# The third matrix of a gated MLP as seven half-size products, and its units streamed from DRAM

## The chip, the cores and the metric

One core of one Trainium2 chip runs the whole program. The metric is device time in microseconds of one launch. Engines as a profile names them: PE (TensorE, matmuls), PEld (its weight loads), DVE (VectorE), ACT (ScalarE), POOL (GpSimd), SP (SyncE, which issues all transfers here).

## The reference, cut to what matters

Three stages run one after the other on 4 batches. Each batch gives 512 tokens and 32 rows of a small state, 544 rows of width 512 in all.

```python
# 1: attention between x (4, 8, 512, 64) and state (4, 8, 32, 64), both ways, concatenated -> (2176, 512)
h = x @ w_in                        # 2: (512 -> 2048)
x = h * tanh(softplus(h)) @ w_out   #    Mish, (2048 -> 512)
xn = x / rms(x) * rms_g             # 3: RMS norm, then a gated MLP
g, val = xn @ w_gate, xn @ w_val    #    (512 -> 1536) twice
out = (g * sigmoid(g) * val) @ w_out2   # (1536 -> 512)
```

The MLP matrices arrive as 64-bit floats, the result is 32-bit.

## The kernel before, in words

**Numbers.** Every operand of a large product is kept as two 16-bit halves, a high and a low one, after a power-of-two scale. A product is three matmuls: high·high, high·low, low·high. A weight is loaded as 64-bit words, put together on DVE and ACT, measured (`norms`: squares on ACT), scaled by `pow2` (one tiny PE matmul against `ones`, line 468, and six tiny DVE operations), and split (`split`: high on either engine, low on DVE, line 590).

**Tiling.** Tokens run in five chunks: four of 512 columns (c = 0 to 3) and one of 128 (c = 4, the state rows of all batches). Matrices are cut into units of 512 of the inner width: u = 0 to 3 in the Mish MLP (`group`, `l2`: groups g0 to g8), u = 0 to 2 in the gated one.

**Gated MLP.** For each chunk and unit, `quad` computes the gate product and then the value product. Each is a 512 x 512 by 512 x 512 product, done as seven products of 256 x 256 blocks instead of eight: weight blocks W11, T2, T1, T3, W21, W22, T4 (and W12 for the small chunk), token blocks A11, S2, S1, A12, S3, A22, S4. One such half-size product is 12 matmuls of 256 columns (line 1088). Three banks of PSUM (pool `p`, four banks) are used per quad, one of them three times; five DVE additions (line 1100) combine them. Then ACT takes Silu (line 1126), DVE multiplies by the value (line 1134), and the result is split into a high part (`gh`, line 457 or 455) and a low part (`gl`, line 1138).

**The last matrix** (w_out2, `w2`) is `l3`, line 1200: for each unit, four output banks `a0` to `a3`, each 12 matmuls of 512 columns, accumulated over the three units. Before, all of `w2` lies in SBUF.

**Weights on the way.** The gate and value matrices are prepared during the Mish MLP in a region of `psm`, then stored to DRAM (`keep`) and loaded back (`load`) to where they stay: unit 0 in `attm`, unit 1 in `w1`, unit 2 in `w2m`, `w2` in `psm`. `attm` is attention's memory, `w1` and `w2m` hold the Mish matrices until these are done.

**Order.** Nothing is issued in the order of the code. Each step is an `op` with its reads, writes, engine choices and an assumed cost; `Plan.order` runs a list schedule over them, ten times, and each engine's instructions are then emitted in that order. `at` and `due` are due times that `chains` spreads backwards, and pools (`p`, `t`, `g`, `a0` ...) limit how far one step may be ahead of another. On the chip the order is fixed: an instruction that is not ready holds up all behind it on its engine. This holds for PE and for SP's one queue of transfers as well.

Of the kernel before, what the change touches and what calls it, by code (L numbers as in the profile page):

```python
# [22 lines left out]
XX, XW, XN, XK = 15, 14, 9, 22  # L23
# [8 lines left out]
class Op:  # L32
    __slots__ = (
        "engs", "fn", "deps", "succ", "bufs", "tab", "at", "due", "reserve", "lat", "name", "spare")


class Plan:
# [15 lines left out]
    def __init__(self, nc):  # L53
        self.nc, self.spare = nc, None
# [14 lines left out]
    def op(self, engs, fn, r=(), w=(), tab=None, at=None, reserve=0, lat=0.0, after=(), due=None, name=""):  # L69
        o = Op()  # L70
        o.engs, o.fn, o.tab, o.at, o.due, o.reserve, o.lat, o.name = engs, fn, tab, at, due, reserve, lat, name
        o.spare = self.SPARE if self.spare is None else self.spare
# [69 lines left out]
    def chains(self):  # L142
# [7 lines left out]
        for o in reversed(self.ops):  # L150
            cost = min(o.engs.values())
            cost = cost + o.lat if "T" in o.engs else (1.0 if "D" in o.engs else o.spare) * cost + o.lat
# [164 lines left out]
def attn_moe_moe_kernel(  # L317
# [74 lines left out]
    prep = Mem("", 0, psm, 2048)  # L392

    home, rest = {}, {}
# [16 lines left out]
    P.fifo.update(("t", "g", "xb", "xt", "t2", "t3", "sbt"))  # L411
    P.pool("t", [tt(512 * k, 512) for k in range(10)])
    P.pool("g", [gm(512 * k, 512, F16).rearrange("p (l f) -> p l f", l=2) for k in range(6)])
    P.pool("sx", [sxm(512 * k, 512) for k in range(2)])
# [4 lines left out]
    P.pool("raw2", stage[:1])  # L419
    sb = attm(0, 2048).rearrange("p (b g h d) -> p b g h d", b=B, g=2, h=4)  # L420
# [23 lines left out]
    def part(w, u, j, a):  # L444

        m, at = rest[w, u] if j == 7 else (home[w, u][0], home[w, u][1] + 512 * j)
        return m(at + 256 * a, 256, F16)

    def part_names(w, u, js):
        m, at = home[w, u]  # L450
        return [n for j in js for n in (rest[w, u][0].names(rest[w, u][1], 512) if j == 7 else m.names(at + 512 * j, 512))]
# [12 lines left out]
    def pow2(part, pname, k, floor, nm, xexp):  # L464
# [4 lines left out]
           r=[pname], w=[b], reserve=0, name=f"pow2 {nm}")  # L469
        t, q, s, si = small([128, k]), small([128, k], I32), small([128, k]), small([128, k])  # L470
        z = small([128, k], I32)

        def fn(e):
            nc.vector.tensor_scalar(t, P[b][:, :k], floor, 2.0, ALU.max, ALU.mult)
# [6 lines left out]
        op({"V": 0.93}, fn, r=[b], w=[(nm, "s")], name=f"pow2 {nm}")  # L481
# [84 lines left out]
    def norms(pairs, nm, xexp, who):  # L566


        part, tot = small([128, 2]), small([128, 1])
        for i, (ap, ns) in enumerate(pairs):  # L570
            q = buf(fresh("junk"), "junk")

            def fn(e, i=i, ap=ap, q=q):
                nc.scalar.activation(  # L574
                    P[q].rearrange("p (a n) -> p a n", a=2), ap, ACTF.Square, accum_out=part[:, i:i + 1])

            op({"A": a_sb(1024) + 0.17}, fn, r=ns, w=[q, (nm, "n", i)], name=f"sq {who}")
        op({"V": 0.13}, lambda e: nc.vector.tensor_tensor(tot, part[:, 0:1], part[:, 1:2], ALU.add),
           r=[(nm, "n", 0), (nm, "n", 1)], w=[(nm, "t")])
        return pow2(tot, (nm, "t"), 1, 2.0 ** -10, nm, xexp)[0]  # L580
# [12 lines left out]
    def plain(w, u, m, at, xexp, pool="raw", after=()):  # L593
# [4 lines left out]
        def dn(k):  # L598
# [4 lines left out]
                   for i in range(2)], (w, u), xexp, f"{w}{u}")  # L603
# [6 lines left out]
    def seven(w, u, m, at, pool, after=()):  # L610
# [18 lines left out]
        for k in range(4):  # L629
# [3 lines left out]
        def both(a, b):  # L633
            return m(at + 256 + 512 * a, 512 * (b - a + 1)).rearrange("p (x f) -> p x f", f=512)[:, ::b - a, :]

        s = norms([(both(W11, W12), qn(W11, W12)), (both(W21, W22), qn(W21, W22))], (w, u), XW, f"{w}{u}")
# [17 lines left out]
    def state_scale():  # L654
# [10 lines left out]
        s, si = pow2(part, "xpart", B, 2.0 ** -50, "x", XX)  # L665
# [159 lines left out]
    def sread_scale(due):  # L825
# [7 lines left out]
        s, si = pow2(part, "x4part", 1, 2.0 ** -50, "x4", XX)  # L833
# [284 lines left out]
    def gated(c):  # L1118
        oa = [buf(("oa", c, t), f"a{t}") for t in range(4)]
        for u in range(U2):  # L1120
            c3, kap = sc[f"c3{u}"], sc[f"kap{u}"]
            A, c12, c21, c22 = quad(c, u, "wg")
            s11 = buf(fresh("s"), "t")
            ss = []
            for k, (i, o) in enumerate(((A, s11), (c12, c12), (c21, c21), (c22, c22))):
                op({"A": a_ps(512) + 0.09}, lambda e, i=i, o=o, c3=c3: nc.scalar.activation(  # L1126
                    P[o], P[i], ACTF.Silu, scale=c3), r=[i, f"c3{u}"], w=[o], tab="silu", name="silu")
                ss.append(o)
            flush2()
            vs = quad(c, u, "wv")  # L1130
            gs = []
            for s, v in zip(ss, vs):
                g = buf(fresh("g"), "g")
                op({"V": v1(512) + 0.06}, lambda e, s=s, v=v, kap=kap: nc.vector.scalar_tensor_tensor(
# [232 lines left out]
```

## Time and profile before

| | |
|---|---|
| median of 3 runs | 810.72 us (808.15 to 813.57) |
| the profiled execution, its own time | 811.83 us |
| its span, first to last instruction | 810.1 us |
| PE busy | 784.5 us (97%), 5362 matmuls |
| DVE busy | 596.1 us (74%) |
| ACT busy | 373.9 us (46%) |
| mean granted TensorE clock | 0.981 |
| moved by the transfers | 76.86 MB |

An engine that is busy 97% of the span need not be the bound everywhere, and an idle engine is not free where one of its results is awaited. So the rows below go stage by stage: how busy each engine is there, what PE waited for, and how long one operation takes when the next follows at once.

### The profile page before, as it was taken

What the parts mean: (1) busy time and instruction counts of PE and PEld (TensorE: products, weight loads), DVE (VectorE), ACT (ScalarE), POOL (GpSimd) and SP (SyncE); (2) the same over time, 40 slices, a digit from 0 to 9 for tenths busy, and PEclk for the clock granted to TensorE, in tenths of its full rate; (3) what the DMA queues carried; (4) which work ended last, traced back from release to release, by engine and by line L of the source; (5) the groups of instructions that cost most, each with busy time, mean ns of one, the idle gap of its engine ahead of it and who ended that gap; (6) DMA issues with size and microseconds to landing.
All of it is one profiled execution on the core that took longest, in us unless ns stands there. A gap on an engine that the chain in (4) does not pass through costs nothing.

```text
span 810.1 us, 13000 instructions
## 1 busy us (share of the span) xinstructions
PE 784.5 (97%) x5362; PEld 481.5 (59%) x5362; DVE 596.1 (74%) x1237; ACT 373.9 (46%) x617; POOL 1.6 (0%) x7
## 2 busy tenths in 40 slices
PE   6799999999999999999999999999999999999996
PEld 4344454544444445754457767776776777777673
DVE  5999999989998868688556896458666784645532
ACT  6999898943644635556444542113410340211200
POOL 0000000000000000000000000000000000000000
PEclk9589999999999999999999999999999999999998
DMA  8654614102242731525473210011001000010010
GB/s 221 206 158 156 228 48 142 53 1 108 101 179 120 299 154 55 209 104 195 156 286 143 86 72 1 1 53 53 1 2 53 27 1 1 2 53 1 1 40 27
DMA packets 31983, 76.86 MB, mean 95 GB/s; under 512 B 19508, under 2 KB 19508, under 8 KB 29108
## 3 DMA queue, kind: packets, MB, share of 16 engines
q1 hardware_dynamic: 31924, 76.03, 26.7%
q8 instruction: 42, 0.69, 0.3%
q14 instruction: 17, 0.14, 0.0%
HBM read 55.84 MB, written 20.19 MB: 94 GB/s over the span
## 4 chain that ended last, share of the span: by engine, by line
PE 69%; DVE 12%; ACT 9%; DMA 8%; issue 1%; SPq 0%; ACTq 0%; DVEq 0%
PE p L1088 27%; PE a L1200 16%; PE a L940 11%; PE p L903 9%; DMA psm<-in_moe_w_out_dram 3%; PE p L1166 2%; ACT sxm L549 2%; DVE psm L590 2%; DMA psm<-in_moe_w_gate_dram 1%; DMA psm<-in_moe_w_val_dram 1%; ACT junk L574 1%; DVE g L918 1%; DVE psm L459 1%; DMA kept_wg<-psm 1%; PE a L1266 1%
## 5 line engine op out<-in xcount | busy, mean ns | idle before, releaser
L940 PE MATMUL a<-g,w2m 128*128 128x512 f16 (+1 forms) x960 | 185.7, 347 | 0.4 <-ACT slot L455 0.4
L903 PE MATMUL p<-slot,w 128*128 128x512 f16 (+1 forms) x960 | 184.7, 348 | 0.0
L1100 DVE TENSOR_TENSOR tt<-p,tt 128x512 f32<-128x512 f32 x120 | 82.5, 689 | 80.4 <-PE p L1088 79.8
L903 PEld LDWEIGHTS <-w 128*128 128x128 f16 x960 | 85.6, 98 | 91.5 <-issue 2.9
L1200 PE MATMUL a<-psm,g 128*128 128x512 f16 x612 | 138.0, 379 | 0.0
L940 PEld LDWEIGHTS <-w2m 128*128 128x128 f16 x960 | 85.7, 99 | 87.8 <-issue 3.1
L1200 PEld LDWEIGHTS <-g 128*128 128x128 f16 x612 | 59.7, 98 | 64.5
L1088 PEld LDWEIGHTS <-w2m 128*128 128x128 f16 x672 | 65.7, 98 | 11.3
L1088 PEld LDWEIGHTS <-w 128*128 128x128 f16 x672 | 65.7, 98 | 11.2 <-issue 1.7
L1088 PEld LDWEIGHTS <-attm 128*128 128x128 f16 x672 | 65.7, 98 | 10.3
L914 ACT ACTIVATE tt<-p,page 128x512 f32<-128x512 f32 x68 | 45.6, 673 | 32.6 <-PE p L903 32.4
L455 ACT ACTIVATE g<-tt 128x512 f16<-128x512 f32 x24 | 14.7, 626 | 89.2 <-PE a L1200 45.5
L918 DVE SCALAR_TENSOR_TENSOR g<-tt,page,g 128x512 f16<-128x512 f32 x68 | 50.7, 748 | 3.0 <-ACT g L455 2.1
L590 DVE SCALAR_TENSOR_TENSOR psm<-psm,page 128x512 f16<-128x512 f32 x60 | 45.0, 750 | 4.3 <-ACT psm L455 2.1
L1126 ACT ACTIVATE tt<-tt,page 128x512 f32<-128x512 f32 x36 | 25.9, 721 | 47.6 <-DVE tt L1100 47.6
L549 ACT ACTIVATE sxm<-psm 128x512 uint16<-128x512 uint16 x58 | 43.4, 773 | 9.6 <-DMA psm<-in_moe_w_out_dram 6.0
L1088 PE MATMUL p<-slot,attm 128*128 128x256 f16 x384 | 46.5, 273 | 0.0
L1088 PE MATMUL p<-slot,w2m 128*128 128x256 f16 x384 | 46.3, 273 | 0.0
L1088 PE MATMUL p<-slot,w 128*128 128x256 f16 x384 | 46.0, 273 | 0.0
L455 ACT ACTIVATE psm<-psm,page 128x512 f16<-128x512 f32 (+1 forms) x37 | 26.2, 717 | 30.4 <-DVE psm L590 23.4
L544 DVE TENSOR_SCALAR sxm<-psm 128x512 uint16<-128x512 uint16 x68 | 28.2, 453 | 11.8 <-DMA psm<-in_moe_w_out_dram 7.5
L1138 DVE TENSOR_TENSOR g<-tt,g 128x512 f16<-128x512 f32 x48 | 31.9, 689 | 1.3 <-ACT g L455 0.2
(182 smaller groups left out, 906.5 us busy)
## 6 DMA issues: line engine op xcount, KB each, us to landing
psm<-in_moe_w_out_dram SPq DMA_DIRECT2D x14, 1024.0 KB, 5.0
psm<-in_moe_w_in_dram SPq DMA_DIRECT2D x8, 1024.0 KB, 5.3
psm<-in_moe_w_gate_dram SPq DMA_DIRECT2D x6, 1024.0 KB, 5.2
psm<-in_moe_w_val_dram SPq DMA_DIRECT2D x6, 1024.0 KB, 5.2
kept_wg<-psm SPq DMA_DIRECT2D x3, 2048.0 KB, 7.0
kept_wv<-psm SPq DMA_DIRECT2D x3, 2048.0 KB, 7.9
out_dram<-slot SPq DMA_DIRECT2D x4, 1024.0 KB, 3.8
attm<-in_x_dram SPq DMA_DIRECT2D x24, 128.0 KB, 3.1
```

The costliest lines, as they stand in the source:

```text
L455: nc.scalar.activation(o, i, ACTF.Copy, scale=1.0 if scale is None else scale)
L544: nc.vector.tensor_scalar(s16[:, :, 1], r16[:, :, 3], 0x8000, None, ALU.bitwise_and)
L549: nc.scalar.activation(s16[:, :, 0], r16[:, :, 1], ACTF.Copy, scale=2.0 ** -13, bias=2.0 ** -14 - 0.5)
L590: op({"V": v1(512)}, lambda e: nc.vector.scalar_tensor_tensor(lo, f, s, h, ALU.mult, ALU.subtract), r=[*fn_, *hn, sname], w=ln, name=f"sl ...
L903: nc.tensor.matmul(P[ph][:, i * n:(i + 1) * n], part("wi", u, k, a)[:, f * 128:(f + 1) * 128], xh[:, k, b, :], start=m == 0, stop=m == 3 * ...
L914: op({"A": a_ps(512) + 0.09}, lambda e, s=s, ph=ph, ce=ce: nc.scalar.activation(P[s], P[ph], ACTF.Mish, scale=ce), r=[ph, f"ce{c}_{u}"], w ...
L918: op({"V": v1(512) + 0.06}, lambda e, s=s, g=g, u=u: nc.vector.scalar_tensor_tensor(P[g][:, 1, :], P[s], rho[u], P[g][:, 0, :], ALU.mult, ...
L940: nc.tensor.matmul(P[ya[d]][:, :n], part("wo", u, f, a)[:, d * 128:(d + 1) * 128], P[g][:, b, i * n:(i + 1) * n], start=first and m == 0, ...
L1088: nc.tensor.matmul(P[to][:, f * 256:f * 256 + 256], part(w, u, j, a)[:, k * 256 + f * 128:k * 256 + f * 128 + 128], h[:, k, b, :], start=b ...
L1100: op({"V": v1(512) + 0.06}, lambda e: nc.vector.tensor_tensor(P[to], P[bank_], P[a], ALU.add), r=[bank_, a], w=[to], name=f"{w} add")
L1138: op({"V": v1(512)}, lambda e, s=s, g=g: nc.vector.tensor_tensor(P[g][:, 1, :], P[s], P[g][:, 0, :], ALU.subtract), r=[s], w=[g], name="gl")
L1200: nc.tensor.matmul(P[oa[t]], P[g][:, a, o:o + 128], part("w2", u, f, b), start=first and m == 0, stop=last and m == 11)
```

## The change

**Seven products for the last matrix.** `w2` is prepared like the gate and value units (`seven`: four block sums and eight splits per unit, where `plain` had four splits). After a unit's value product, `value` forms the seven token blocks of the result: four DVE additions or subtractions (`less`) and seven splits, where there were four. The first three block products (`first_three`) accumulate over the units in banks a0 to a2, and their token parts are dropped. The other four blocks' parts are kept for all three units of a chunk, in 14 buffers of `w2m` (pool `g2`). When the next chunk's gate of unit 0 has been queued, `finish` adds the other four products to the three banks, unit after unit, with DVE taking sums out in between, and stores the chunk. A block product is 12 matmuls of 256 columns (`lprod`).

**Homes.** `w2m` is now taken by those parts, so gate and value units 0 and 2 share `w1`, and unit 1 shares `attm` with four of the seven blocks of every `w2` unit. All of these are loaded from DRAM again in every chunk. The blocks for the small chunk (W12) go to the slots of finished chunks.

**Preparation.** A second region (`prep2`, in `attm`) is used beside the first; `floor` holds these steps back to set times (`KEEP0`, `KSTEP`). `norms` now squares a unit in eight groups of 256 columns for each partition, where it had two of 1024. The small chunk's products are mixed into chunk 3, and its result is stored ahead of the last half of chunk 3's.

```diff
-XX, XW, XN, XK = 15, 14, 9, 22
+XX, XW, XN, XK = 15, 13, 9, 22
...
+            if o.floor is not None:
+                late[o] = max(late[o], o.floor)
...
-    for n, m in enumerate((attm, w1, w2m)):
+    for n, m in enumerate((w1, attm, w1)):
         home["wg", n], home["wv", n] = (m, 0), (m, 3584)
-    for u in range(U2):
-        home["w2", u] = (psm, 2048 * u)
+
+    def spot(w, u, j):
+
+        if j == 7:
+            k = ("wg", "wv", "w2").index(w) + 3 * u
+            return slotm[k // 4], k % 4 * 512
+        if w == "w2":
+            return (psm, 1536 * u + 512 * j) if j < 3 else (attm, 2048 * u + 512 * (j - 3))
+        m, at = home[w, u]
+        return m, at + 512 * j
...
+    P.pool("g2", [w2m(512 * k, 512, F16).rearrange("p (l f) -> p l f", l=2) for k in range(14)])
...
+        less(s1, a21, a22, ALU.add)
+        block("A11", a11, "g")
+        less(s2, s1, a11)
+        block("S2", s2, "g")
+        block("S1", s1, "g")
+        block("A12", a12, "g2")
+        less(a21, a11, a21)
+        block("S3", a21, "g2")
+        block("A22", a22, "g2")
+        less(a12, a12, s2)
+        block("S4", a12, "g2")
+        return gs
+
+    def lprod(to, g, u, j, begin=False):
+
+        def fn(e):
+            for t in range(2):
+                for f in range(2):
+                    for a, b in ((0, 0), (0, 1), (1, 0)):
+                        o = f * 256 + t * 128
+                        nc.tensor.matmul(
+                            P[to][:, t * 256:t * 256 + 256], P[g][:, a, o:o + 128],
+                            part("w2", u, j, b)[:, f * 256:f * 256 + 256],
...
+    def first_three(c, u, gs, oa):
+        for to, nm, j in zip(oa, ("A11", "S2", "S1"), (W11, T2, T1)):
+            lprod(to, gs[nm], u, j, u == 0)
...
+        def over(to, nm, j):
+            for u in range(U2):
+                lprod(to, gss[u][nm], u, j)
...
+        scaled(lambda: two(P[a1]), [a1], A)
+        add(lambda: two(P[u2]), [u2], B_, a1)
+        over(B_, "S3", T3)
+        add(lambda: two(P[u3]), [u3], B_, a1)
+        over(A, "A12", W21)
+        scaled(lambda: c11[0], c11[1], A)
+        add(lambda: c22[0], c22[1], C, u3)
+        over(C, "S4", W22)
+        add(lambda: c12[0], c12[1], C, u2)
+        for f in between:
+            f()
+        over(B_, "A22", T4)
+        add(lambda: c21[0], c21[1], B_, a1)
...
+            for u in range(U2):
+                ss = gate(c, u)
+                if c == B - 1:
+                    sb_ = small_gate(u)
+                if u:
+                    first_three(c, u - 1, gss[u - 1], oa)
+                elif before is not None:
+                    first_three(c - 1, U2 - 1, before[0][-1], before[1])
+                    finish(c - 1, *before)
+                    load("wg", 1)
+                    load("wv", 1)
+                    if c + 1 >= B - 1:
+                        load_rest(c - B + 2)
+                gss.append(value(c, u, ss))
+                if c == B - 1:
+                    small_gs.append(small_value(u, sb_))
+                if u == 0:
+                    load("wg", 2)
+                    load("wv", 2)
+                elif u == 1:
+                    for v in range(U2):
+                        load("w2", v, 1)
+                elif c + 1 < B:
+                    load("wg", 0)
+                    load("wv", 0)
...
+KEEP0, KSTEP = (100, 200), 36
+LATER = 40
```

**Where it moves instructions.** First, SP's queue in the gated MLP. Names: `w_69` is `w1`; `kept_wg_106`, `_108`, `_111` are gate units 0, 1, 2; `kept_wv_107`, `_110`, `_112` are the value units after (`_107`, `_109`, `_112` before); `slot_76` is chunk 0's. Before, from the last load of a whole unit on:

```order
L1248 DMA w2m<-kept_wv_112 128x3584
L1241 DMA kept_w_115<-psm 128x2048
L1248 DMA psm<-kept_w_114 128x2048
L1248 DMA psm<-kept_w_115 128x2048
L1222 DMA out_dram<-slot_76 128x2048
L1257 DMA slot_76<-kept_wg_106 128x512
```

And now, for chunk 1's gate and value units:

```order
L1385 DMA w_69<-kept_wg_106 128x3584
L1385 DMA w_69<-kept_wv_107 128x3584
L1385 DMA w_69<-kept_wg_111 128x3584
L1385 DMA attm<-kept_wg_108 128x3584
L1385 DMA w_69<-kept_wv_112 128x3584
L1385 DMA attm<-kept_wv_110 128x3584
L1385 DMA attm<-kept_w_113 128x2048
L1252 DMA out_dram<-slot_76 128x2048
```

Before, nothing but results and the small chunk's blocks follow the first chunk. Now nine loads of 1792 or 1024 KB stand in the queue for each chunk, in the order of their releases by PE.

Second, PE at the start of chunk 1, where the last product that reads `w2` blocks below the new home of gate unit 1 ends (`a_88` is bank a1, `p_86` a bank of a quad):

```order
L1195 LDWEIGHTS w2m
L1195 MATMUL a_88<-attm,w2m 128x256
L1111 LDWEIGHTS w_69
L1111 MATMUL p_86<-w_69 128x256
```

From this place five further block products of value unit 0 and one of the last matrix follow, 72 matmuls of 256 columns, and then the first matmul that reads gate unit 1 out of `attm`. The load of that unit can only run under these 72.

Third, DVE after the value products of a unit. Before, of chunk 1:

```order
L1134 SCALAR_TENSOR_TENSOR tt<-tt,page_116 128x512
L1100 TENSOR_TENSOR tt<-p_84,tt 128x512
L1134 SCALAR_TENSOR_TENSOR tt<-tt,page_116 128x512
L1100 TENSOR_TENSOR tt<-p_86,tt 128x512
L1134 SCALAR_TENSOR_TENSOR tt<-tt,page_116 128x512
L457 CAST g<-tt 128x512
L1138 TENSOR_TENSOR g<-tt,g 128x512 x3
```

And now, of the same chunk (1173 is `less`, 1154 the low part, 1225 a sum taken out by `finish`):

```order
L1162 SCALAR_TENSOR_TENSOR tt<-tt,page_114 128x512
L1173 TENSOR_TENSOR tt<-tt 128x512 x3
L1154 TENSOR_TENSOR w2m<-tt,w2m 128x512
L1123 TENSOR_TENSOR tt<-p_84,tt 128x512
L1225 SCALAR_TENSOR_TENSOR slot_76<-a_88,page_114,tt 128x2x256
L1154 TENSOR_TENSOR w2m<-tt,w2m 128x512
L1154 TENSOR_TENSOR g<-tt,g 128x512 x2
L1123 TENSOR_TENSOR tt<-p_84,tt 128x512
L1173 TENSOR_TENSOR tt<-tt 128x512
L1154 TENSOR_TENSOR w2m<-tt,w2m 128x512 x2
```

Additions that free a bank for PE (1123) now stand between the block sums and the low parts of the unit before.

## Rows read from the trace of the kernel before

**Rows 1.** The page: busy us of the span, then busy tenths in 40 slices.
```profile
PE 784.5 (97%) x5362; PEld 481.5 (59%) x5362; DVE 596.1 (74%) x1237; ACT 373.9 (46%) x617; POOL 1.6 (0%) x7
...
PE   6799999999999999999999999999999999999996
...
DVE  5999999989998868688556896458666784645532
```

**Rows 2.** Windows: us, then PE, PEld, DVE, ACT, POOL busy (instructions), clock, DMA share, GB/s.
```profile
0.00:80.00 80.00, 66.52 (x405) 35.90 (x406) 68.64 (x171) 71.31 (x135) 1.59 (x7) 0.83 0.62 187
...
160.00:260.00 100.00, 100.00 (x470) 45.55 (x469) 90.89 (x220) 48.16 (x73) 0.00 (x0) 1.00 0.24 89
260.00:340.00 80.00, 80.00 (x587) 45.07 (x586) 57.85 (x113) 41.25 (x64) 0.00 (x0) 1.00 0.49 186
340.00:420.00 80.00, 76.03 (x436) 38.37 (x434) 60.30 (x130) 43.53 (x69) 0.00 (x0) 1.00 0.51 187
420.00:800.00 380.00, 380.00 (x2956) 277.08 (x2955) 240.56 (x399) 97.79 (x147) 0.00 (x0) 1.00 0.09 35
640.00:660.00 20.00, 20.00 (x139) 13.32 (x138) 19.12 (x33) 8.63 (x17) 0.00 (x0) 1.00 0.00 1
```

**Rows 3.** The chain that ended last, pieces of PE: start us, us, what.
```profile
514.27 9.17 PE p L1088 x84
...
528.65 5.18 PE a L1200 x24
...
563.39 1.31 PE p L1088 x12
...
794.40 7.78 PE a L1200 x36
```

**Rows 4.** Waits of PE after 80 us: line, releaser: us, times, longest; then the last one.
```profile
PE p L468 <- DVE page L578: 4.0, 3, 1.5
...
401.97 0.38 PE L468 MATMUL p<-page,ones 128*128 128x1 f32 x2 [1.49 <-DVE page L578]
```

**Rows 5.** DVE by form from 430 us: count, busy us, mean ns; then its timeline.
```profile
L1100 DVE TENSOR_TENSOR tt<-p,tt 128x512 f32<-128x512 f32 x120 | 82.5, 689 | 80.4 <-PE p L1088 79.8
...
L1134 DVE SCALAR_TENSOR_TENSOR tt<-tt,page 128x512 f32<-128x512 f32 x36 | 26.9, 750 | 2.9 <-DVE tt L1100 0.5
...
642.25 0.75 DVE L1134 SCALAR_TENSOR_TENSOR tt<-tt,page 128x512 f32<-128x512 f32 x1
642.92 0.68 DVE L1100 TENSOR_TENSOR tt<-p,tt 128x512 f32<-128x512 f32 x1
...
646.71 2.49 DVE L1005 SCALAR_TENSOR_TENSOR slot<-slot,rms 128x512 f32<-128x512 f32 x4
```

**Rows 6.** Transfers: count, KB each, median us from issue to landing; then one on SP's timeline.
```profile
kept_wg<-psm SPq DMA_DIRECT2D x3, 2048.0 KB, 7.0
...
out_dram<-slot SPq DMA_DIRECT2D x4, 1024.0 KB, 3.8
...
attm<-kept_wv SPq DMA_DIRECT2D x1, 1792.0 KB, 10.7
...
w2m<-kept_wg SPq DMA_DIRECT2D x1, 1792.0 KB, 7.3
...
w2m<-kept_wv SPq DMA_DIRECT2D x1, 1792.0 KB, 7.5
...
404.35 0.34 SPq L1248 DMA_DIRECT2D w2m<-kept_wg  x1
```

**Rows 7.** Windows, as in Rows 2, of four us with transfers throughout.
```profile
412.00:416.00 4.00, 4.00 (x29) 2.66 (x28) 0.69 (x1) 0.00 (x0) 0.00 (x0) 1.00 1.00 320
```

**Rows 8.** The chain, a piece of ACT: the square and its sum, of 1024 columns.
```profile
400.57 1.16 ACT junk L574 x2
```

**Rows 9.** The end: DVE and SP on the timeline, then what SP waited for.
```profile
802.21 0.75 DVE L459 TENSOR_SCALAR slot<-a,page 128x512 f32<-128x512 f32 x1 [5.76 <-PE a L1200]
803.02 0.68 SPq L1226 DMA_DIRECT2D out_dram<-slot  x1
...
SPq L1363 <- DMA out_dram<-slot: 5.3, 1, 5.3
```

More of the change, by code (lines that the diff above doesn't have):

```diff
@@ L1184, in gated_last, with fn @@
-        flush2()
-    def l3(c, u, gs, oa):
-        ot = slot[c]
-        first, last = u == 0, u == U2 - 1
+        p = bank()
+        def fn(e):
+            for f in range(4):
+                m = 0
+                for k in range(KD):
+                    for a, b in ((0, 0), (0, 1), (1, 0)):
+                        o = k % 2 * 256 + f % 2 * 128
+                        nc.tensor.matmul(
+                            P[p][:, f * n:(f + 1) * n], part(w, u, js[k // 2][f // 2], a)[:, o:o + 128], xh[:, k, b, :],
+                            start=m == 0, stop=m == 3 * KD - 1)
+                        m += 1
@@ new lines, in small_product, with small_gate @@
+        cost = pe(n, 48)
+        op({"T": cost}, fn, r=[*xr, *part_names(w, u, (W11, W12, W21, W22))], w=[p, "l1"],
+           at=clock[0], name=f"{w} c{c} u{u}")
+        clock[0] += cost
+        return p
+    def small_gate(u):
+        c3 = sc[f"c3{u}"]
+        p = small_product("wg", u)
+        s = buf(fresh("s"), "t")
+        op({"A": a_ps(512) + 0.09}, lambda e: nc.scalar.activation(
+            P[s], P[p], ACTF.Silu, scale=c3), r=[p, f"c3{u}"], w=[s], tab="silu", name="silu")
+        return s
@@ new lines, in small_end @@
+            cost = pe(256, 24)
+            op({"T": cost}, fn, r=[g, *part_names("w2", u, (W11, W12, W21, W22))], w=[oa], at=clock[0], name=f"l3 c{B} u{u}")
+            clock[0] += cost
+        sl = [nm for k in range(KD) for nm in sl_names(B, k)]
+        of = ot.rearrange("p k n -> p (k n)")
+        op({"A": a_ps(512) + 0.09, "V": v1(512) + 0.06}, lambda e: copy_to(e, of, P[oa], osc),
+           r=[oa, "osc"], w=sl, name="end copy")
+        op({"D": 0.73}, lambda e: nc.sync.dma_start(
+            out=out.rearrange("(b r) d -> b r d", b=B)[:, S:, :], in_=of), r=sl, lat=1.9, name="out")
@@ new lines, in attn_moe_moe_kernel, with keep @@
+    kept = {}
+    def keep(w, u, k, after):
+        region, pool = ((prep, "raw2"), (prep2, "raw3"))[k]
+        P.floor = lambda at=T0 + KEEP0[k] + KSTEP * sum(x == k for x in turns): at
+        turns.append(k)
+        t = dram.tile([128, 4096], F32, name=f"kept_{w}{u}")
+        kept[w, u] = t
+        seven(w, u, region, 0, pool, after)
+        op({"D": 5.9}, lambda e: nc.sync.dma_start(out=t[:, :], in_=region(0, 4096)),
+           r=region.names(0, 4096), w=[("kept", w, u)], lat=1.9, name=f"keep {w}{u}")
+        P.floor = None
@@ new lines, in attn_moe_moe_kernel, with load, load_rest @@
+    turns = []
+    def load(w, u, k=0, after=()):
+        j, n = (0, 7) if w != "w2" else ((0, 3), (3, 4))[k]
+        m, at = spot(w, u, j)
+        op({"D": n * 512 / 690}, lambda e: nc.sync.dma_start(
+            out=m(at, n * 512), in_=kept[w, u][:, j * 512:(j + n) * 512]),
+            r=[("kept", w, u)], w=m.names(at, n * 512), lat=1.9, after=after, name=f"back {w}{u}")
+    def load_rest(last):
+        for k, (w, u) in enumerate((w, u) for u in range(U2) for w in ("wg", "wv", "w2")):
+            if (k // 4 > B - 3) != last:
+                continue
+            m, at = spot(w, u, W12)
+            op({"D": 0.74}, lambda e, w=w, u=u, m=m, at=at: nc.sync.dma_start(
+                out=m(at, 512), in_=kept[w, u][:, 3584:]), r=[("kept", w, u)], w=m.names(at, 512),
+                lat=1.9, name=f"rest {w}{u}")
@@ L1317, in attn_moe_moe_kernel @@
         flush()
-        for u in range(1, U2):
-            load("wg", u)
-            load("wv", u)
-        rms(1, slots_xe[1])
-        gated(0)
-        rms(2, slots_xe[0])
-        gated(1)
-        rms(3, slots_xe[1])
-        rms(B)
-        gated(2)
-        load_rest()
-        gated(3)
-        gated_last()
+        load("wg", 0)
+        load("wv", 0)
+        opened.append(op({"X": 0.01}, lambda e: None, w=w2m.names(0, 7168), name="open"))
+        opened.append(op({"X": 0.01}, lambda e: None, w=psm.names(4608, 1792), after=[conv], name="open"))
+        P.floor = lambda: clock[0] - LATER
+        gated()
         P.run()
@@ L1337 @@
 LEAD = 0
-KEEP = 1.0
+KEEP0, KSTEP = (100, 200), 36
+LATER = 40
 DUE2, DUE3 = 30, 30
```

304 lines of the change are left out of this document (143 added, 161 removed).

## The prediction

> **What bounds the kernel now.** I read the slices first: PE is busy in nine tenths or more of every slice from the third to the last but one [rows 1]. A busy share hides what kind of busy, so the windows by stage come next: from 160 to 340 us and from 420 to 800 us PE is busy for all of the time, at a granted clock of 1.00 [rows 2]. In the gated MLP nothing but PE's own work sets the pace: DVE has 240.6 us of work in those 380. What PE loses lies in the first 80 us (13.5 us idle, at a mean clock of 0.83), between 340 and 420 us (4.0 us), and behind the last matmul. The list of waits names the 4.0 us: three times PE stood at the tiny matmul of a weight's scale, up to 1.5 us, because the chain of load, conversion and squares came late [rows 4]. So a change that takes work from PE gains all of it, as long as no new wait appears.
>
> **PE's work.** The chain gives clean prices, since its pieces of PE are back to back. 24 matmuls of 512 columns of line 1200 take 5.18 us, 216 ns each; 84 of 256 columns of line 1088 take 9.17 us, 109.2 ns each; a block product of 12 is 1.31 us [rows 3]. A unit of a large chunk costs 48 x 216 ns = 10.36 us in the last matrix before, and 7 x 12 x 109.2 ns = 9.17 us after. Twelve unit-chunks save 14.3 us. The small chunk's 36 matmuls (7.78 us) become 72 narrow ones (7.86 us). **Net -14.2 us**, all on PE's path.
>
> A rule speaks against this. By the rows, halving the columns halves the time. The Trainium skill (TensorE: Matmul & The Clock Gate, Back-to-back issue gap) gives for a sustained stream of weight loads and matmuls some 81 ns at 128 columns and 131 ns at 512. An estimate between these puts 256 columns near 98 ns, so that 576 wide matmuls would cost 75 us and 1008 narrow ones 99 us, and the change would lose 23 us. The trace disagrees (216 and 109.2 ns), and the sum goes by the trace.
>
> **DVE in the gated MLP.** Each unit-chunk gains four block sums and three low parts, seven operations of the 689 ns kind. A mean duration overstates a queue that is full: four such operations follow each other in 2.49 us, a step of 0.60 us, and one with a scalar has a step of 0.67 (642.25 to 642.92) [rows 5]. So 12 x 7 x 0.60 = 50 us, and some 5 us for the sums of the outputs: about 296 us in 366, 81%. It lies beside PE's work. The densest place is units 1 and 2 of a chunk, which also carry the next chunk's norm: I count 64 plain operations and 10 with a scalar against 37 block products. By steps that is 45.1 us of DVE in 48.5 of PE. In a window of 20 us of the kernel before DVE was busy for 19.1 and PE lost nothing [rows 2], so 93% can be carried. I take **+0.5 us**; the bounds are 0 and the second case below.
>
> **Preparation.** w2 gains per unit four sums and four low parts on DVE, 3 x (4 x 0.60 + 4 x 0.67) = 15 us. Between 160 and 420 us DVE idles for 51 us [rows 2], which covers it; were the cover gone, it would cost up to 15. Squares: two of 1.16 us a unit [rows 8] become eight of a quarter of the size. The same columns at least (2.3 us), at most eight times a half of 1.16 (4.6), so up to 2.3 us more before each scale. ACT has room, but PE stands at that scale's tiny matmul if it is late. Six such matmuls come late in the Mish MLP now. The price of one wait is 1.3 us (4.0 over 3) [rows 4]; the bounds are -4.0 (none left) and +5. I take one or so more: **+1.5 us**.
>
> **From one MLP to the other.** The order puts the store of w2's last-but-one unit, a load of 1792 KB into w1 and the load of gate unit 1 behind one another, the last into memory that the store still reads. PE has 3 block products, 11 pieces of six wide matmuls (1.30 us each) and one more of the norm to do meanwhile, some 18.7 us. The store takes 7.0 us and the load 7.3 to 10.7 [rows 6]; the load between them moves 1.84 MB, 5.7 us at 320 GB/s [rows 7]. Fully one after the other that is 20.0 to 23.4 us, overlapped it is 14.3. Bounds 0 and +4.7; I take **+1.5 us**.
>
> **Loads at each chunk's edge.** Three loads have little time: gate unit 0, gate unit 1 and value unit 1, each before chunks 1, 2 and 3. The work that the order leaves PE between release and first use is six block products, 7.87 us, in five of the nine, 8.4 to 9.4 in three, and 13 in one. A load of this size with little beside it landed in 7.3 and 7.5 us, with others beside it in up to 10.7 [rows 6]. Here the one before it was released 9.2 us or more earlier, so I take the former rows: they fit by 0.4 us, and for the way over SP and back I take **+1.0 us** in all. Bounds: 0, and 19.3 if all land in 10.7. Behind a waiting load on SP stand only loads and stores that are needed a unit later or more.
>
> By the Trainium skill (DMA: Bandwidth & Descriptors, Anatomy of one DMA) a transfer costs about 2.0 us and its bytes at 436 GB/s, an estimate of 6.2 us here. By that figure the 1.0 us falls away; the trace's 7.3 us is nearer the edge and stays in the sum.
>
> The other loads of a chunk (gate and value unit 2, value unit 0, w2's second parts) have a dozen or more block products, 16 us. In all some 14 MB a chunk, 150 GB/s over 90 us, against 320.
>
> **Head and end.** The first 80 us hold the same work in a somewhat different order: 0, bounds +-2, a seventh of the idle time there. At the end DVE and one transfer follow the last matmul as before, 512 KB where there were 256; the 1024 KB ones landed in 3.8 us, the last one was awaited 5.3 [rows 6, 9]. I take 0, with -1.5 and +1 as bounds.
>
> **Sum.** -14.2 + 0.5 + 1.5 + 1.5 + 1.0 = -9.7 us. The profiled execution took 811.8 us, so 802.1; it lies 1.1 us above the median of 810.7, so **801.0 us**.
>
> **Rivals.** *DVE becomes the bound in the dense stretches* (0.18). If operations cost their mean durations there, 64 x 0.689 + 10 x 0.750 = 51.6 us, and DVE also waits as it did in that window (0.88 us of 20, so 2.2), the stretch of 49.0 us of PE (with the norm's own matmul) lasts 53.8. Three such stretches give back 14.4 us, all of the gain; waits for loads then hide in them, and 1.5 us of scale waits remain: 811.8 - 14.2 + 14.4 + 1.5 = 813.5, by the median 812.4. For it: the queue's order is fixed, so a late addition holds a bank and PE behind it. Against it: the steps of 0.60 us. It decides once DVE's steps there exceed 0.65 us.
>
> *The loads land late* (0.10). With 10.7 us each at the edges and in the transition: -14.2 + 19.3 + 4.7 + 1.5 + 0.5 = +11.8, 822.5 by the median, **slower** by 1.5%. For it: two of the rows are above 10 or near it when transfers share the engines. Against it: at the edges they mostly run alone. It decides from a landing of about 9.6 us.
>
> *The narrow matmuls of the last matrix do not hold 109 ns* (0.02), since their stationary side now comes fresh from DVE's buffers: each ns more costs 1.0 us, and at 123 ns the gain is gone (815 with the waits). The figure of the Trainium skill above is of this kind. Nothing in the rows of line 1088, which load weights as often, is for it.
>
> **Numbers.** The forecast has 0.70. About 1% (8.1 us) is what a measurement of this kernel can tell from no change, so faster means below 802.6: of the forecast 0.53, of the second case 0.02, **0.55**. Within 1%: 0.17 of the forecast, 0.16 and 0.02, **0.35**. Slower: **0.10**. The range runs from 796, where every new wait is absent, to 810, which leaves out most of the two slow cases.
>
> **What would show it.** Right: line 1195 at 109 ns for each matmul, 110 us in all; PE idle below 6 us between 420 us and its end; DVE near 80% there. The edge loads in 7 to 8 us with PE waits under 1 us each. Wrong: PE waiting on DVE's additions for microseconds in units 1 and 2 (second case); PE waiting on a load into attm or w1 by 2 us and more, nine times (third); scale matmuls awaited for over 5 us in all, or the start of the first gate product later than its share of the work says. Then the terms taken as 1.5 us were the ones that failed.

## The result, and the profile after

The changed kernel took **800.45 us** (median of 4 runs, 798.95 to 801.31); the kernel before took 809.84 beside it. The ratio is 0.9876, with a 95% interval from 0.9836 to 0.9916. The forecast was 801.0. The sum was met, but its terms for the preparation, the head and the end were each missed by 2.9 us or more, and these errors cancelled.

The profiled execution took 801.31 us, its span is 799.5 us, against 811.83 and 810.1. I cut both spans at two events that stand at the same place of the work. The first is the group of eight matmuls of 64 x 512 of attention 2 that lies between products of the Mish MLP (line 776, now 799): PE has the same work before it in both kernels (busy behind it for 575.5 us and 561.6, 13.9 us apart, where the change takes 14.2 from the work there). The second is the last DVE operation. First the row of before on PE's timeline (start us, us, line), then its two rows of after, on PE's and DVE's timeline:

```profile
222.73 1.99 PE L776 MATMUL p<-tt,attm 64*128 64x512 f32 x8
```
```profile
231.32 1.99 PE L799 MATMUL p<-tt,attm 64*128 64x512 f32 x8
...
794.49 0.75 DVE L1225 SCALAR_TENSOR_TENSOR slot<-a,page,tt 128x512 f32<-128x512 f32 x1 [3.18 <-PE a L1195]
```

| piece, us | before | after | difference |
|---|---|---|---|
| head: start to the marker | 222.7 | 231.3 | +8.6 |
| middle: marker to the last DVE operation | 579.5 | 563.2 | -16.3 |
| end: from there to the span's end | 7.9 | 5.0 | -2.9 |
| span | 810.1 | 799.5 | -10.6 |

The page answers to [rows 1]: less PE time in more matmuls, DVE from 74% to 81%, and in the slices DVE is busier in the gated MLP, where the new sums stand.

```profile
PE 772.9 (97%) x5830; PEld 528.0 (66%) x5830; DVE 650.1 (81%) x1332; ACT 435.8 (55%) x802; POOL 1.6 (0%) x7
...
PE   7699998999999999999999999999999999999997
...
DVE  5989999998978798897689898668975998666671
```

The windows answer to [rows 2] (us, then PE, PEld, DVE, ACT, POOL, clock, DMA share, GB/s). The first is the kernel before, in a stretch that [rows 2] do not have, and the others are the changed kernel:

```profile
120.00:130.00 10.00, 9.91 (x58) 5.64 (x58) 9.90 (x34) 6.83 (x19) 0.00 (x0) 1.00 0.73 199
```
```profile
0.00:80.00 80.00, 64.84 (x400) 34.44 (x401) 68.31 (x167) 68.88 (x130) 1.59 (x7) 0.85 0.60 173
...
120.00:130.00 10.00, 7.36 (x35) 4.18 (x34) 9.66 (x25) 8.12 (x15) 0.00 (x0) 0.83 0.55 163
...
210.00:220.00 10.00, 8.14 (x31) 3.31 (x30) 9.21 (x25) 6.23 (x19) 0.00 (x0) 0.83 0.15 62
...
340.00:420.00 80.00, 80.00 (x545) 45.10 (x544) 65.43 (x135) 48.83 (x102) 0.00 (x0) 1.00 0.39 149
420.00:788.00 368.00, 366.43 (x3379) 318.28 (x3377) 282.87 (x469) 133.53 (x216) 0.00 (x0) 1.00 0.48 177
...
620.00:640.00 20.00, 20.00 (x186) 17.93 (x184) 19.80 (x33) 13.69 (x22) 0.00 (x0) 1.00 0.73 277
```

Read them as three findings. The 4.0 us that PE lost between 340 and 420 us are gone. From 420 to 788 us it loses 1.6 us in 368, while DVE is busy for 77% there and for 19.80 us of 20 in the densest place, without PE losing anything. And two windows of the head, full before but for 0.1 us, now hold idle time at a clock of 0.83. The waits of PE after 80 us name all of it (line, releaser: us, times, longest), in answer to [rows 4]:

```profile
PE p L739 <- ACT tt L937: 2.6, 2, 1.5
PE p L481 <- ACT junk L599: 1.9, 1, 1.9
PE p L1111 <- DMA attm<-kept_wg: 1.3, 3, 0.6
PE p L926 <- ACT tt L937: 0.3, 1, 0.3
PE p L1111 <- DVE tt L1123: 0.2, 1, 0.2
```

The third is the load of gate unit 1 at each chunk's edge: the cost forecast at 1.0 us is 1.3. The second is a scale (line 481, 468 before) that waits for the squares (line 599). PE's timeline shows what stands behind that wait, and ACT's what stands ahead of it (the first and the last of the eight squares; each has its sum read out behind it):

```profile
213.76 0.39 PE L481 MATMUL p<-page,ones 128*128 128x8 f32 x2 [1.86 <-ACT junk L599]
214.01 7.03 PE L926 MATMUL p<-slot,w 128*128 128x512 f16 x24
...
208.99 0.42 ACT L599 ACTIVATE junk<-psm 128x256 uint8<-128x256 f32 x1
209.31 0.19 ACT L599 ACTIVATION_READ_ACCUMULATOR junk<-psm 128x1 f32 x1
...
213.20 0.42 ACT L599 ACTIVATE junk<-psm 128x256 uint8<-128x256 f32 x1
213.52 0.19 ACT L599 ACTIVATION_READ_ACCUMULATOR junk<-psm 128x1 f32 x1
```

The squares take from 208.99 to 213.71, with one other operation of ACT between them, and 24 matmuls behind the wait take 7.03 us where the same 24 take 5.34 elsewhere: part of them ran at 1.2 GHz, the lower level, which the text below calls the half clock.

The chain's pieces of PE answer to [rows 3]: 36 matmuls of the last matrix in 3.93 us are 109.2 ns each.

```profile
454.24 1.31 PE a L1195 x12
...
510.57 3.93 PE a L1195 x36
```

The transfers (count, KB each, median us from issue to landing), in answer to [rows 6]:

```profile
w<-kept_wg SPq DMA_DIRECT2D x8, 1792.0 KB, 7.2
...
attm<-kept_wg SPq DMA_DIRECT2D x4, 1792.0 KB, 8.2
attm<-kept_wv SPq DMA_DIRECT2D x4, 1792.0 KB, 8.7
...
out_dram<-slot SPq DMA_DIRECT2D x2, 512.0 KB, 3.0
```

### The profile page after: what moved, and what is told of

Read it like the earlier page. It is cut to its first block, busy times and chain, and to the rows that moved or that the text cites. A ratio compares the mean times of both kernels' runs of the same rounds, so it can differ in the third digit from the quotient of the medians.

```text
span 799.5 us, 14253 instructions
## 1 busy us (share of the span) xinstructions
PE 772.9 (97%) x5830; PEld 528.0 (66%) x5830; DVE 650.1 (81%) x1332; ACT 435.8 (55%) x802; POOL 1.6 (0%) x7
## 4 chain that ended last, share of the span: by engine, by line
PE 71%; DVE 16%; DMA 6%; ACT 6%; issue 1%; DVEq 0%; ACTq 0%; SPq 0%
PE p L1111 25%; PE a L963 14%; PE p L926 13%; PE a L1195 12%; DMA attm<-kept_wg 3%; PE p L1271 2%; ACT junk L599 1%; DVE g L941 1%; DVE w2m L612 1%; PE a L1309 1%; DVE sxm L562 1%; DVE page L507 1%; PE a L1403 1%; DMA kept_wg<-psm 1%; ACT sxm L567 1%
## 5 line engine op out<-in xcount | busy, mean ns | idle before, releaser
L926 PEld LDWEIGHTS <-w 128*128 128x128 f16 x960 | 86.3, 99 | 90.3 <-issue 4.1
L1111 PEld LDWEIGHTS <-w 128*128 128x128 f16 x1344 | 131.3, 98 | 17.0 <-issue 0.3
L1111 PE MATMUL p<-slot,w 128*128 128x256 f16 x768 | 93.3, 273 | 0.0
L468 ACT ACTIVATE w2m<-tt 128x512 f16<-128x512 f32 x45 | 26.9, 623 | 93.0 <-DVE tt L1162 81.1
L1111 PEld LDWEIGHTS <-attm 128*128 128x128 f16 x672 | 65.4, 98 | 10.6 <-DMA attm<-kept_wg 2.2
L1195 PE MATMUL a<-attm,w2m 128*128 128x256 f16 x576 | 66.2, 273 | 0.0
L1195 PE MATMUL a<-psm,g 128*128 128x256 f16 x432 | 51.9, 273 | 0.0
L1195 PEld LDWEIGHTS <-g 128*128 128x128 f16 x432 | 42.2, 98 | 5.6 <-issue 0.6
L1154 DVE TENSOR_TENSOR w2m<-tt,w2m 128x512 f16<-128x512 f32 x48 | 32.2, 686 | 0.9 <-ACT w2m L468 0.6
L1173 DVE TENSOR_TENSOR tt<-tt 128x512 f32<-128x512 f32 x48 | 32.2, 686 | 0.4
L567 ACT ACTIVATE sxm<-psm 128x512 uint16<-128x512 uint16 x41 | 30.9, 776 | 1.1 <-DVE w2m L578 0.6
L612 DVE SCALAR_TENSOR_TENSOR psm<-psm,page 128x512 f16<-128x512 f32 x40 | 29.9, 748 | 1.2 <-ACT psm L468 0.3
```

Of the source, the lines that this page charges most:

```text
L468: nc.scalar.activation(o, i, ACTF.Copy, scale=1.0 if scale is None else scale)
L567: nc.scalar.activation(s16[:, :, 0], r16[:, :, 1], ACTF.Copy, scale=2.0 ** -13, bias=2.0 ** -14 - 0.5)
L612: op({"V": v1(512)}, lambda e: nc.vector.scalar_tensor_tensor(lo, f, s, h, ALU.mult, ALU.subtract), r=[*fn_, *hn, sname], w=ln, name=f"sl ...
L926: nc.tensor.matmul(P[ph][:, i * n:(i + 1) * n], part("wi", u, k, a)[:, f * 128:(f + 1) * 128], xh[:, k, b, :], start=m == 0, stop=m == 3 * ...
L1111: nc.tensor.matmul(P[to][:, f * 256:f * 256 + 256], part(w, u, j, a)[:, k * 256 + f * 128:k * 256 + f * 128 + 128], h[:, k, b, :], start=b ...
L1154: op({"V": v1(512)}, lambda e: nc.vector.tensor_tensor(P[g][:, 1, :], P[s], P[g][:, 0, :], ALU.subtract), r=[s], w=[g], name="gl")
```

## The experiments

They are read like the table above; each kernel has 1206 or 1207 matmuls ahead of the marker. All head and middle figures are from one profiled execution each; the ratios are against runs of the kernel before on the same chip. Up to the marker, experiments 1 to 4 hold the same instructions in the same order as the changed kernel, and yet their heads lie between 227.9 and 230.8 us, against its 231.3. So a head of one execution is good to some 3 us.

| kernel | median us | ratio, 95% | head | middle | end |
|---|---|---|---|---|---|
| after | 800.45 | 0.9876 [0.9836, 0.9916] | 231.3 | 563.2 | 5.0 |
| 1 eighth product | 812.03 | 1.0013 [1.0000, 1.0025] | 230.1 | 575.9 | 5.0 |
| 2 no reloads | 798.54 | 0.9851 [0.9831, 0.9870] | 230.8 | 561.5 | 5.2 |
| 3 gate unit 1 twice | 827.54 | 1.0212 [1.0191, 1.0234] | 227.9 | 591.0 | 4.9 |
| 4 more DVE work | 824.78 | 1.0174 [1.0148, 1.0200] | 230.8 | 588.1 | 5.0 |
| 5 before, new norms | 821.71 | 1.0146 [1.0128, 1.0165] | 232.1 | 578.4 | 7.9 |
| 6 after, old norms | 797.15 | 0.9844 [0.9827, 0.9860] | 225.1 | 565.2 | 5.1 |
| 7 split loads | 797.09 | 0.9839 [0.9825, 0.9854] | 225.7 | 562.8 | 5.2 |
| 8 two squares | 795.75 | 0.9829 [0.9815, 0.9844] | 225.9 | 563.2 | 5.0 |
| 9 old norms, split loads | 799.53 | 0.9862 [0.9841, 0.9883] | 226.4 | 565.6 | 5.2 |
| 10 two squares, split loads | 795.32 | 0.9806 [0.9787, 0.9824] | 226.3 | 561.8 | 5.2 |

**1. Is the gain PE's?** The work that the change saved is put back, one more block product for each unit, into a bank that holds nothing at that time.

```diff
+            if again and not dummy:
+                fn(e, True)
```

> An eighth block product is put back: the first block product of every unit but the very first is computed once more into an unused bank, 11 x 12 = 132 matmuls of 256 columns, with the order of all else unchanged and the result unused. Theory (PE's work alone sets the pace of the gated MLP): 132 x 109.2 ns = 14.4 us more, less at most the 1.3 us of waits for loads that it may hide, so 813.5 to 815 us against 800.5, and no longer faster than before. Rival (part of the gated MLP is paced by DVE or by loads, so that PE's saving is only worth a part): 10 us or less, 810 us or below.

The middle grew by 12.7 us for 132 matmuls. At 109.2 ns they are 14.4; the edge waits fell from 1.3 to 0.6, and the other 1 us I cannot place. The time, 812.03 us (809.64 to 813.37), lies 1.5 us below what was expected and 2.0 above the rival's 810; the head came out 1.2 us shorter. The theory is the nearer one: 12.7 of the 14.4 us came back, so PE's own work sets nearly all of the pace of the middle. The kernel is no faster than the one before then (1.0013).

**2. Are the loads hidden?** The reloads of chunks 1 to 3 are left out.

```diff
-                    load("wg", 1)
-                    load("wv", 1)
+                    load("wg", 1, skip=True)
+                    load("wv", 1, skip=True)
```

> Left out: all loads of gate, value and last-matrix units after those of chunk 0 (27 loads of 1024 or 1792 KB), so that chunks 1 to 3 are computed with whatever lies in the homes; nothing else is changed. Theory (a load costs only what PE is seen to wait for it, 1.3 us in all): 1 to 1.5 us less, about 799 us. Rival (42 MB of traffic also slows the engines or the other transfers): 4 us less or more, 796.5 us or below.

The middle fell by 1.7 us, the wait for `kept_wg` is gone from the list, and no other took its place. 27 loads cost little more than the 1.3 us that their waits on PE showed, and the rival's 4 us are not there.

**3. What if they were late?** Gate unit 1 is loaded twice at each edge.

> At the start of chunks 1, 2 and 3 the load of gate unit 1 is issued twice, one after the other, into the same place. Theory (the load fits under the six block products between release and use by some 0.1 us, so a second landing lies wholly on PE's path): three times 7.2 to 8.2 us, 21.5 to 24.5 us more, 822 to 825 us. Rival (there is slack that the order does not show, or PE makes the time up later): less than 8 us more, below 808.5 us.

The list of PE's waits, and one of the three places on PE's timeline:

```profile
PE p L1111 <- DMA attm<-kept_wg: 23.5, 3, 7.9
...
537.01 2.74 PE L1111 MATMUL p<-slot,attm 128*128 128x256 f16 x12 [7.79 <-DMA attm<-kept_wg]
539.54 1.64 PE L1111 MATMUL p<-w,attm 128*128 128x256 f16 x12
541.02 1.47 PE L1195 MATMUL a<-attm,w2m 128*128 128x256 f16 x12
```

Each lateness arrives on PE whole: 7.8 us a wait, the time of one more load. The middle grew by 27.8 us, of which 22.2 are the waits. The rest is the clock: the 12 matmuls after the wait took 2.74 us instead of 1.47, and windows of 100 us that had 1.00 show 0.95 to 0.97. So there was no slack at the edge, as expected, but a late load is dearer than its wait: 827.54 us lies 2.5 above the top of what was expected.

**4. Does DVE have room?** 48 more operations of the 689 ns kind, at the sums and the low parts of S1 and S2, in the same order.

> Four operations of DVE are issued twice in each unit (the first two block sums, the low parts of two blocks), 48 operations at a step of 0.60 us, 28.8 us more of DVE's work in the gated MLP, in the same order. Theory (DVE still has room: the densest stretch grows from 45.1 to 49.9 us of DVE against 48.5 to 49.0 of PE, and elsewhere there is more): 0 to 2 us for each of three stretches, 1 to 5 us in all, 801.5 to 805.5 us. Rival (DVE is already at its edge in the dense stretches): the whole of 4.8 us in each and more, 14 us or above, 814.5 us. A second rival (ample slack): no change within 0.5 us.

My theory fell, the rival was right. 48 steps of 0.60 us are 28.8 us of DVE; the middle grew by 24.9. First the page, then the waits, then two neighbouring windows of this kernel and a third:

```profile
PE 777.9 (94%) x5830; PEld 527.4 (64%) x5830; DVE 681.2 (83%) x1380; ACT 435.8 (53%) x802; POOL 1.6 (0%) x7
...
PE p L1111 <- DVE tt L1123: 12.7, 14, 2.0
PE a L1196 <- DVE tt L1226: 3.1, 2, 1.7
PE p L1111 <- ACT tt L1147: 1.7, 3, 0.6
...
590.00:605.00 15.00, 11.45 (x104) 9.95 (x103) 14.69 (x25) 5.95 (x11) 0.00 (x0) 1.00 0.34 123
605.00:610.00 5.00, 5.00 (x48) 4.49 (x47) 1.28 (x2) 1.30 (x2) 0.00 (x0) 1.00 0.83 301
650.00:670.00 20.00, 17.97 (x160) 15.33 (x158) 19.79 (x34) 7.50 (x17) 0.00 (x0) 1.00 0.51 177
```

PE waited for the addition that frees a bank 14 times, and for sums and Silu that came late behind it. While it loses 3.55 us between 590 and 605, DVE is busy for 14.69 us of 15, and behind that DVE is idle for 3.7 us of 5 while PE is full. The third window shows the same: DVE at 99%, PE short by 2.0 us. So the second case's mechanism is real: DVE is the bound, not over the whole stretch but in the 15 to 20 us of it in which its work is bunched. The order of each queue is fixed, so DVE cannot put off the sums and low parts that stand ahead of the freeing addition, and the idle time behind comes too late. The waits behind 420 us are 20.6 us in all, against 1.5 in the changed kernel; the other 5.8 us of the 24.9 I cannot place. The change's own seven operations a unit just fit. That another order would have fitted these as well was not tried.

**5 and 6. Where does the head's 8.6 us come from?** The new `norms` alone in the kernel before, and the old `norms` in the kernel after (both get an order drawn anew).

```diff
-        for i, (ap, ns) in enumerate(pairs):
+        for i, (ap, ns) in enumerate(groups):
...
-XX, XW, XN, XK = 15, 14, 9, 22
+XX, XW, XN, XK = 15, 13, 9, 22
```

> One part of the change alone, in the kernel before: the norms of gate and value units from eight squares of 256 columns instead of two of 1024 (and the scale exponent 13). Theory (the eight squares of 4.3 us instead of 2.3 make scales late, and PE stands at their tiny matmuls): 2 to 10 us slower, 812.5 to 820 us, with scale waits above the 4.0 us of before. Rival (the first 230 us are slower because of the new order there, not because of the squares): within 1.5 us of the kernel before.

> The changed kernel with the norms of the kernel before (two squares of 1024 columns and a sum, exponent 14), so that the whole order is drawn up anew. Theory (of the 8.6 us that the changed kernel loses up to 230 us, some 3.5 come from the scale wait at 212 us and the low clock behind it, the rest from the order of the first 130 us): 3 to 4 us less, 796.5 to 797.5 us. Rival (all 8.6 us come with the norms, which stand in the way of attention's work from the start): 8 us less, 792 us. Third: the squares cost nothing that the order doesn't hide, 800.5 us.

The norms alone lengthened the kernel before by 1.46%, more than the top of what was expected, with nearly all of it in the head: +9.4 us, as much as the whole change did there. PE's waits for the squares in that kernel after 80 us:

```profile
212.38 0.39 PE L468 MATMUL p<-page,ones 128*128 128x8 f32 x2 [1.85 <-ACT junk L586]
353.79 0.39 PE L468 MATMUL p<-page,ones 128*128 128x8 f32 x2 [1.28 <-ACT junk L586]
386.92 0.38 PE L468 MATMUL p<-page,ones 128*128 128x2 f32 x2 [1.95 <-ACT junk L586]
```

Only the first of the three lies in the head. The rest of what PE loses there after 80 us, 4.3 us, are waits between 112 and 146 us for other operations of DVE and ACT, and the clock was 1.00 throughout. So 1.85 us of the +9.4 are a wait for the squares. How much of the rest is the order that the planner drew for them, and how much ACT's longer work on them ahead of its other operations, is not told apart here.

With the old norms the changed kernel's head is 225.1, 6.2 us less: after 80 us PE stands for 1.9 us there instead of 4.8, and the clock is 1.00. So most of the loss in the head goes with the norms' part of the change and the order drawn for it. The remaining 2.4 us over the kernel before are no more than one execution differs from another, so that the seven products and the loads have none of it is likely, but not shown. The time, 797.15, is in the expected range; the middle gave 2 us back (PE idles there for 3.2 us instead of 1.6, with a scale wait of 0.8 at 378 us and one of 0.6 for DVE).

**7. The edge's loads, cut.** Gate and value units are loaded as blocks 0 and 1, then 2 to 6, so that a first use waits for less.

```diff
+            for j, n in ((0, 2), (2, 5)):
+                load_blocks(w, u, j, n, after)
+            return
```

> The loads of whole gate and value units in the gated MLP are cut in two: the first two blocks (512 KB) by themselves, then the other five (1280 KB). Theory (PE waits 1.3 us for gate unit 1 because the whole unit must land before its first block is used): these waits go, 1.3 us less, about 799 us. Rival (two transfers cost more of the queue than the wait is worth): 800.5 us or up to 3 us more, with waits at the second piece instead.

The edge waits fell from 1.3 to 0.6 us (`kept_wg` and `kept_wv` 0.3 each), but two waits for DVE (0.6 and 0.4) came in their place, and the middle fell by 0.4 only, of the 1.3 expected. The rest of the 3.4 us is in the head, where the planner drew another order for DVE, ACT and SP, though not for PE: the scale wait there was 1.22 us, with no lower clock behind it. It is no fruit of the loads.

**8. The squares, with the order held.** The planner sees eight squares and orders for them; two of 1024 columns are issued. So only ACT's work changes.

> The changed kernel in exactly its own order, but of a unit's eight squares only two are issued, each of 1024 columns, where the fourth and the eighth stood (POOL sets the unused sums to zero). Theory (the last square of the second gate unit comes some 2 us earlier, and the wait of 1.9 us at 212 us, with the stretch at 1.2 GHz behind it, goes): 3.0 to 4.0 us less, 796.5 to 797.5 us. Rival (the wait hangs on the transfer of that unit, not on ACT's squares): less than 1 us.

It took 4.7 us less by the medians (795.08 to 797.13 against 798.95 to 801.31), more than expected, and the head 5.4. Its row for the scale, its window there, and then the same place in experiment 3, which has all eight squares:

```profile
210.07 0.39 PE L481 MATMUL p<-page,ones 128*128 128x8 f32 x2 [0.51 <-ACT junk L605]
...
210.00:220.00 10.00, 9.93 (x47) 4.65 (x48) 9.19 (x24) 4.55 (x8) 0.00 (x0) 1.00 0.00 1
```
```profile
212.00 0.39 PE L481 MATMUL p<-page,ones 128*128 128x8 f32 x2 [1.77 <-ACT junk L599]
212.24 5.34 PE L926 MATMUL p<-slot,w 128*128 128x512 f16 x24
```

The wait fell by 1.35 us (the squares end 2.4 us after the first starts, not 4.7), a wait of 0.3 us at 151 us is gone too, and so is the half clock behind the scale, 1.7 us. Only the waits are surely the squares' own. In experiment 3 the same eight squares made PE wait for 1.77 us, and the 24 matmuls behind took 5.34 us, at full clock; its head, 227.9, is 1.9 us above this one. So the squares cost some 1.9 us of the head, and 1.7 more where the clock fell behind their wait. The other 2 us of the head lie before 200 us, most of them a stretch at the lower clock behind two waits at 124 us that this kernel has as well (1.49 and 1.13 us), at a clock of 1.00. That part is not the squares' doing.

**9 and 10. Both put together.**

> The changed kernel with two things put together that were run apart: each weight's norm again from two squares of 1024 columns, and the gate and value units' loads of the gated MLP cut into blocks 0 and 1 and blocks 2 to 6. If what is left of the loss lies in the head (order and waits up to the first matmul of attention 2 with 512 columns) and the loads cost only the waits seen at the chunks' edges, the two add up little: the old norms stood at 797.15 with 1.5 us of edge waits, so 795.5 to 797 us, with edge waits of 0.3 to 0.6 us. Rival: both gains come from the head alone, where only one of them can be had, and the split buys nothing: 797 to 798 us.

> The split loads with two of the eight squares issued, each of 1024 columns, and the rest of the program in the order of the kernel with split loads. If the eight squares are what lengthens the wait for a scale, and so the stretch at half clock behind it, then this kernel loses what that kernel still waits there: its wait of 1.22 us at 209.83 us falls to about 0.3, no half clock was there to lose, so 796 us, from 795.3 to 797. Rival: the squares were only worth the half clock, and with it gone nothing is left to gain: 797 us.

Kernel 9 missed both expectations, at 799.53. Its PE waits of the middle (first from the marker to 420 us, then from there on) show why:

```profile
PE p L481 <- DVE page L591: 1.6, 2, 1.0
...
PE a L1185 <- DVE g L1144: 0.6, 2, 0.3
PE p L1101 <- DVE sxm L1054: 0.4, 1, 0.4
```

The planner, given other costs, drew an order in which two scales come late again. By the windows PE idles for 2.9 us in this middle and for 1.6 in that of kernel 7. The other 1.5 us of the difference are time in which PE counts as busy, though 4625 matmuls stand behind the marker in both; I cannot place them. The head is longer all the same, at a clock of 1.00 from 80 us on. So an order alone is worth 2 to 3 us here, as much as these edits can gain.

Kernel 10 keeps the order of kernel 7, and its scale wait is 0.4 us, as expected. The time is in the expected range: **795.32 us**, ratio 0.9806 [0.9787, 0.9824], the lowest median here and 0.6% below the changed kernel, though not told apart from experiment 8. But its head, 226.3, is no shorter than kernel 7's 225.7, so these two profiles do not show where the 1.8 us between the medians come from.

## Why the prediction was right, and where it was not

**PE's work, -14.2 us: right.** 109.2 ns for each narrow matmul, and experiment 1 gave back 12.7 us for one block product in all units but the first. The estimate from the Trainium skill (TensorE: Matmul & The Clock Gate, Back-to-back issue gap), near 98 ns and a loss of 23 us, was rightly set aside: the rows of line 1195 disagree with it as those of before did.

**DVE, +0.5: right in size (0.2), wrong in its reason.** The forecast counted steps of 0.60 us against PE's time over a stretch of 48.5 us and found 3.4 us of room. The steps are right. But DVE's work is not spread evenly over the stretch: at 620 us it is busy for 19.80 us of 20, and has no room left there. Experiment 4 shows what that means: 48 operations more, which by the count overrun PE by some 1 us in each of three stretches, cost 24.9 us. What had to be counted is DVE's work in the 15 to 20 us in which it is bunched, and how late it makes the addition that frees a bank. The second case named that mechanism; its threshold of 0.65 us a step rests on the same count and was the wrong quantity.

**Preparation, +1.5 with -4.0 as a bound: at the bound in the middle.** The three late scales of before are gone, -4.0 us, and none came after 260 us. The change holds these steps to other times and uses a second region, and the order that came of it had them early; which of the two did it was not tried. The forecast took one or so more late scales. There was one, but in the head, together with its half clock.

**From one MLP to the other, +1.5: nothing.** No wait there. The store was issued at 436.5 us and landed after 7.3, the load of gate unit 1 followed at 443.8, and PE first read it at 455.4, without a wait. So the cover, 18.7 us by the forecast and 18.9 here, was enough.

**Loads at the edges, +1.0: 1.3**, three waits of at most 0.6 us. The size is near, but the landing it rests on was not: gate unit 1 took 8.2 us in the median, where the forecast had 7.3 to 7.5 against 7.87 of cover and named 7 to 8 as its sign. The rival of late loads did not come true, and was right in its price: experiment 3 made them late, and each us came to PE, with a clock loss on top. The Trainium skill's figure (DMA: Bandwidth & Descriptors, Anatomy of one DMA) is a fit to transfers that GpSimd issues; all here are issued by SyncE. The estimate of 6.2 us that the forecast took from it was too low for these: 7.2 us into `w1` and 8.2 to 8.7 into `attm`.

**Head, 0 with +-2: +8.6.** This is the term that failed, and it was named "the first 80 us hold the same work in a somewhat different order". The first 80 us cost about 2 us, within the bound (PE idles for 15.2 us there instead of 13.5). The rest came between 80 and 231 us, a stretch the sum had no term for: waits at 124 us, a scale at 213, and the half clock behind each. Most of it goes with the norms: the old ones take 6.2 us off (experiment 6), and the new ones alone add 9.4 (5). With the order held the squares themselves are some 1.9 us of this, and 1.7 more where the clock falls behind their wait (8). How the rest divides between the order drawn for them and the clock behind its waits stays open, the more so as the same instructions took 227.9 us in experiment 3. The squares stood in the forecast with up to 2.3 us for each scale; the sum gave them 1.5 for a count of late scales taken from the Mish MLP's end, and nothing for the clock.

**End, 0 with -1.5: -2.9.** The row of before was a 256 KB store that was awaited for 5.3 us [rows 9]. In the changed kernel the small chunk's result goes out ahead, at 791.4 us, and what remains at the end is 512 KB that land in 3.0. The forecast took the end as unchanged, though two rows it named (1024 KB landed in 3.8 us, 256 KB awaited for 5.3) already say that bytes alone do not set this time.

Together: -14.2 + 0.2 - 4.0 + 0 + 1.3 + 8.6 - 2.9 = -11.0, against -10.6 measured. The forecast of -9.7 came out because the head's +8.6 stood against 5.5 us of scale waits, 1.5 of the transition and 2.9 at the end that did not come. That the total came within 1 us of the forecast is luck to this extent; PE's term, which decides that the kernel is faster, was right for its reason.

## What to carry to other kernels

When an edit changes the assumed costs of a list schedule, every stage is drawn anew: give each stage a term, also those that the edit does not touch, and 2 to 3 us either way here. The room of a second engine in a fixed order is not its idle share over a stage: look for the 15 or 20 us in which it is already full, and for what stands there ahead of the operation that the first engine waits for. Before costing a wait, ask whether PE ran at full clock ahead of it; the stretch behind may cost as much as the wait. And before explaining a few us from one profile, see how far the same instructions differ in another.

## What the runs showed that was not expected

**A short wait of PE may or may not lower the clock.** The scale wait near 213 us stands at the same place in five kernels with the order of after. After 1.86 (after), 1.95 (experiment 1), 1.78 (2) and 1.94 us (4), the window 210:220 shows a clock of 0.83; after 1.77 us (3) it shows 1.00, as it does after 1.85 us in experiment 5, whose order is another. The two waits at 124 us, 1.1 to 1.5 us each, were followed by 0.83 in after and experiment 2, and by 1.00 in experiments 1, 3, 4 and 8. A stretch costs 1.4 to 1.7 us, so such a wait is worth its length or twice that, and which cannot be read from it. What decides stays open. After each of the three waits of 7.8 us in experiment 3 the clock fell.

**Small transfers can be the slow ones.** At the end 256 KB were awaited for 5.3 us before and 512 KB landed in 3.0 after. The kernel before shows what differs, in the window of its last store and in that of the 1024 KB one ahead of it:

```profile
804.30:808.60 4.30, 0.00 (x0) 0.00 (x0) 0.00 (x0) 0.00 (x0) 0.00 (x0) 0.67 0.24 61
788.10:790.80 2.70, 2.70 (x52) 2.70 (x50) 1.23 (x3) 0.00 (x0) 0.00 (x0) 1.00 0.87 355
```

The small store keeps the 16 transfer engines busy for a quarter of the time, at 61 GB/s, and the large one for 0.87, at 355. They differ in shape, and which property makes the difference was not tried.
